# K products of an S4 layer on TensorE: two channels in one 64x66 product instead of one channel in a 32x33 product

## The chip, the cores and the metric

One core of a Trainium2 chip runs the kernel; the other cores are not used. The metric is the device time of one execution in microseconds (us), and runs are compared by their medians. The engines are named as in the profile: PE (TensorE; its weight loads are listed apart as PEld), DVE (VectorE), ACT (ScalarE), POOL (GpSimd) and SP (SyncE, which here only issues DMAs).

## The reference, cut to what matters

The output mixes two branches with a gate: `out = g * a + (1 - g) * b`, for 2048 positions and 640 channels, in bf16. Branch `a` is an S4 layer: for each channel a kernel K of 2048 taps is computed from 128 complex modes, and the input is convolved with it. Branch `b` is a gated MLP with a 2048 x 2048 product over the positions.

```python
    logdA = dt * A                                             # A complex, (D, N) = (640, 128)
    P = jnp.exp(logdA[:, :, None] * l[None, None, :])          # l = 0 .. 2047
    K = jnp.einsum('dn,dnl,dn->dl', Cc, P, dB).real
...
    y = irfft(rfft(pad(u)) * rfft(pad(K)))[:L] + u * Dskip     # convolution, per channel
...
    z1, z2 = split(gelu(x @ w_in)); z2 = layernorm(z2)
    b = (z1 * (w_sp @ z2 + b_sp)) @ w_out
    g = sigmoid((x * gate_w).sum(-1))
```

## The kernel before, in words

K is never evaluated tap by tap. Tap l is split into a coarse and a fine part, so that exp(l * logdA) is a product of two table entries, and the sum over the 128 modes is a matrix product with the modes on the 128 partitions. For one channel the coarse table has 32 rows that are used (real and imaginary parts apart) and the fine table 33. Channel d of K is thus a 32 x 33 block: the real product (`ET[:, 0:32, d]` by `M2[:, :, d]`) plus the imaginary one (`ET[:, NA:NA+32, d]` by `E2[:, :, d]`), accumulated in PSUM.

The channels are processed in eight groups c = 0..7 of 80. For each group:

- `k_exps` (for four groups at a time) and `k_tables` (lines 973 to 1030) fill the tables in the tile `ET{z}`, z = c % 2. It holds E1, E2 and M2 as rows of 80 channels, so the entries of one channel lie 80 elements apart. This is work of DVE and ACT.
- `k_sub` (lines 1034 to 1058) does the products. The 80 channels are four quarters q of 20. A quarter has its own 32 output columns of the PE array (`tile_position=(0, 32 * q)`) and so its own 32 PSUM partitions. For i in 0..19 and q in 0..3 there are two matmuls, lines 1045 and 1046: weights 128x32, moving operand 128x33. That is 160 matmuls, and as many weight loads, for a group, all in one PE task. One PSUM tile `ps_k` (two banks, from the ring "two", which has two such tiles and serves most large products of the kernel) takes all of it. Two copies (lines 1054 and 1056), both on DVE or both on ACT, bring it to the SBUF tile `kf` in order of taps: 17 columns of the fine table one way, 16 in reverse.
- `k_store` (lines 1069 to 1085) adds the skip weights to tap 0 (line 1075) and writes K to DRAM: for each quarter one DMA to `KA_d` and one to `KB_d`, and one more for the last row. It is called for the groups 0 to 3 together, for 4 and 5, and for 6 and 7 (lines 1311, 1312). `kf` of the first six groups (480 channels, h = 0) and of the last two (160 channels, h = 1) is one SBUF tile each.

`k_expand(h)` then reads `KA_d` and `KB_d` with some 27 DMAs, `conv_s1(h)` transforms K, and `conv_s2`, `conv_vt` and `conv_i2` do the convolution. The other branch runs alongside: `sp_block(tb)`, tb = 0..7, is the product over positions (line 812: 128x128 weights, 256 moving columns, 112 matmuls for a block) and the output product (line 832); `z1_tile` (line 624) and `s1_u` (line 651) are further PE work of the same stretch.

The order of the work is written by a planner, class `Plan` (lines 125 to 317). Every task is added with an engine (or a choice of engines), a cost in us, tiles and keys that it reads and writes, and a bias. The planner simulates the engines, always takes the ready task with the largest remaining path plus bias, and emits the instructions in that order; each engine runs its own in that fixed order. The dictionary `TUNE` (lines 38 to 121) adds searched biases to groups of tasks. A K product is entered with a cost of 3.65 and starts in the plan no earlier than 4.0 after the one before it has ended.

Of the kernel before, what the change touches and what calls it, by code (L numbers as in the profile page):

```python
# [25 lines left out]
class Handle:  # L26
# [9 lines left out]


TUNE = {
    ('conv_s1', 15, ('g', 0)): -1398,
    ('conv_s1', 15, None): 3878,  # L40
    ('conv_s2', 35, ('h', 0)): 10715,
    ('conv_s2', 34, ('h', 0)): 12557,
    ('conv_s2', 34, ('h', 1)): 10661,
    ('conv_s2', 28, None): -730,
    ('conv_s2', 42, None): 11507,
    ('eights', 6, None): 22869,
    ('eights', 13, None): 9278,
    ('i2_out', 15, None): 2641,
    ('k_expand', 28, ('h', 1)): -13135,
    ('k_exps', 10, ('c', 4)): -5933,  # L50
    ('k_exps', 10, None): -2461,
    ('k_store', 13, ('h', 1)): -2592,
    ('k_store', 14, None): -14209,
    ('k_store', 6, None): 2313,
    ('k_tables', 31, ('c', 4)): 1745,
    ('k_tables', 31, None): 2593,
    ('k_tables', 32, ('c', 3)): -6618,
    ('k_tables', 32, None): -5389,
    ('k_tables', 41, ('c', 3)): -7569,
    ('k_tables', 29, ('c', 3)): 19395,  # L60
    ('k_tables', 29, ('c', 7)): 107,
    ('k_tables', 29, None): -29059,
    ('k_tables', 6, ('c', 2)): -1107,
    ('k_tables', 6, None): -36,
    ('k_tables', 18, ('c', 5)): 11204,
    ('k_tables', 18, None): 3646,
    ('k_tables', 17, ('c', 3)): -6816,
    ('k_tables', 17, None): 2377,
    ('k_tables', 36, ('c', 0)): 6700,
    ('k_tables', 36, ('c', 7)): -59230,  # L70
    ('k_tables', 36, None): -4043,
    ('k_tables', 38, None): -15448,
    ('main', 151, ('g', 0)): 41152,
    ('main', 151, ('g', 1)): 3118,
    ('main', 151, ('g', 2)): 1052,
    ('main', 149, None): 37766,
    ('main', 148, None): 1429,
    ('main', 147, None): 3632,
    ('main', 156, None): 2671,
    ('main', 159, None): -8713,  # L80
    ('main', 370, None): -17765,
    ('main', 369, None): -1820,
    ('main', 442, None): 125,
    ('main', 445, None): 3317,
    ('main', 413, None): -4292,
    ('quads', 10, None): 798,
    ('s1_u', 13, ('n0', 12)): -14799,
    ('s1_u', 13, ('n0', 2)): -11216,
    ('s1_u', 16, ('n0', 12)): -1100,
    ('s1_u', 16, ('n0', 2)): -2702,  # L90
    ('s1_u', 16, ('n0', 4)): -8304,
    ('s1_u', 16, None): -26814,
    ('s1_u', 20, ('h', 1)): 37644,
    ('s1_u', 3, ('n0', 0)): -28168,
    ('s1_u', 3, None): 2258,
    ('s1_u', 18, ('h', 1)): -33016,
    ('s1_u', 14, None): -24028,
    ('sp_block', 23, ('tb', 4)): -6232,
    ('sp_block', 23, None): 6779,
    ('sp_block', 25, None): 2910,  # L100
    ('sp_block', 20, ('tb', 0)): 13918,
    ('sp_block', 20, None): -32605,
    ('sp_block', 42, ('tb', 4)): -3738,
    ('sp_block', 42, ('tb', 5)): -4450,
    ('sp_block', 47, ('tb', 3)): 6173,
    ('sp_block', 3, ('tb', 1)): -8813,
    ('sp_block', 3, ('tb', 2)): 26644,
    ('sp_block', 3, ('tb', 7)): -26408,
    ('sp_block', 8, None): -13664,
    ('sp_block', 6, None): -1104,  # L110
    ('sp_block', 5, ('tb', 7)): -23479,
    ('sp_block', 5, None): -15147,
    ('tg_build', 15, None): 6085,
    ('tg_build', 20, None): 11595,
    ('x_group', 3, ('g', 0)): -1523,
    ('x_group', 3, ('g', 1)): -4918,
    ('x_group', 3, None): -1876,
    ('z1_tile', 10, ('g', 0)): 17523,
    ('z2_tile', 18, ('h', 1)): -43258,
    ('z2_tile', 10, None): -1119,  # L120
}
HELPERS = ("dma", "actf", "evac", "<lambda>", "ptt", "pts", "ftt", "fts", "pstt", "S_", "E", "K_", "M_")

# [197 lines left out]
def kernel(  # L321
# [20 lines left out]
    P = 128  # L342
# [132 lines left out]
        S_(dma("SP", lambda nm=nm: nat[nm][:], lambda ap=ap: ap, 163840, w=[nm] + (["nat_in"] if k == 3 else []), tr=True, bias=6900 - k))  # L475
    add("DVE", 0.2, lambda e: vec.memset(dsk[:], 0.0), w=["dsk0"], bias=8000)
    for h in range(2):
        dma("POOL", lambda h=h: dsk[0:128:32, (0, 120)[h]:(120, 160)[h]], lambda h=h: A_Dskip[GO[h]:GO[h] + GW[h]].rearrange("(q d) -> q d", q=4), 1000, r=["dsk0"], w=[("dsk", h)], bias=7000)
    dma("POOL", lambda: bs16[:], lambda: B_b_sp.rearrange("(p n) -> p n", n=NS), 4000, w=["bs16"], bias=8000)
    E(dma("SP", lambda: Win1[:], lambda: wiv[:, :, 0:Fh], 1106000, w=["Win1"], r=["nat_in"], bias=3500, run=1728))  # L480

# [550 lines left out]
    SQ = 20  # L1032

    def k_sub(h, s, kf):
        ps = two("ps_k")
        z = s % 2
        tabs = [(nm, z, g) for nm in ("M2p", "E2p") for g in range(2)] + [(nm, z) for nm in ("M2n", "M2z", "E2n", "E2z")] + [(nm, z, g) for nm in ("E1", "E1s") for g in range(3)]

        def m(e):
            ET, M2, E2 = X["ET", z], X["M2", z], X["E2", z]  # L1040
            for i in range(SQ):
                for q in range(4):
                    d = SQ * q + i
                    o_ = ps()[32 * q:32 * q + 32, i // 10, 33 * (i % 10):33 * (i % 10) + 33]
                    pe.matmul(o_, lhsT=ET[:, 0:32, d], rhs=M2[:, :, d], start=True, stop=False, tile_position=(0, 32 * q))  # L1045
                    pe.matmul(o_, lhsT=ET[:, NA:NA + 32, d], rhs=E2[:, :, d], start=False, stop=True, tile_position=(0, 32 * q))  # L1046
        tab_ids.append(add("PE", 3.65, m, r=tabs + (["cva"] if h else []), w=[ps], bias=8000, lag=[(tab_ids[-1], 4.0)] if tab_ids else []))
        pv = lambda: ps()[:, :, 0:330].rearrange("p g (i b) -> p b g i", b=33)
        WQ = GW[h] // 4

        def ev(e):
            cp = vec.tensor_copy if e == "DVE" else act.copy
            kv = kf()[:, 0:33 * WQ].rearrange("p (b d) -> p b d", b=33)
            cp(out=kv[:, 16:33, SQ * s:SQ * s + 20].rearrange("p b (g i) -> p b g i", g=2), in_=pv()[:, 0:17, :, :])
            src = kv[:, 15, SQ * s:SQ * s + 20]
            cp(out=bass.AP(src.tensor, src.offset, [list(src.ap[0]), [-WQ, 16], [10, 2], [1, 10]]), in_=pv()[:, 17:33, :, :])
        i_ = add(("ACT", "DVE"), (0.9, 0.91), ev, r=[ps], w=[(kf, s)], bias=8500)
        K_(h, i_)

    QQ = ("SP", "POOL")  # L1060

# [7 lines left out]
    def k_store(h, kf, s0, s1):  # L1069

        WQ = GW[h] // 4
        c0, c1 = SQ * s0, SQ * s1
        o = (0, 120)[h]
        ks = [(kf, s) for s in range(s0, s1)]
        add("DVE", 0.25, lambda e: vec.tensor_tensor(out=kf()[:, c0:c1], in0=kf()[:, c0:c1], in1=dsk[:, o + c0:o + c1], op=ALU.add),
            r=[("dsk", h)] + ks, w=ks, bias=9000)
        kv = lambda: kf()[:, 0:33 * WQ].rearrange("p (b d) -> p b d", b=33)
        for q in range(4):
            cs = slice(WQ * q + c0, WQ * q + c1)
            r0 = 32 * q  # L1080
            KAB[h] += [("KA", h, q, s0), ("KB", h, q, s0)]
            K_(h, dma(QQ, lambda cs=cs: KA_d[h][:, :, cs], lambda r0=r0: kv()[r0:r0 + 16, :, c0:c1], 1056 * (c1 - c0), r=ks, w=[KAB[h][-2]], bias=8000, run=2 * (c1 - c0)))
            K_(h, dma(QQ, lambda cs=cs: KB_d[h][0:128, cs].rearrange("(a b) d -> a b d", a=4), lambda r0=r0: kv()[r0 + 16:r0 + 20, 0:32, c0:c1], 256 * (c1 - c0), r=ks, w=[KAB[h][-1]], bias=8000, run=2 * (c1 - c0)))
        KAB[h].append(("KC", h, s0))
        K_(h, dma(QQ, lambda: KB_d[h][128, :].rearrange("(q d) -> q d", q=4)[:, c0:c1], lambda: kv()[19:128:32, 32, c0:c1], 640, r=ks, w=[KAB[h][-1]], bias=8000))

    def k_expand(h):
        W = GW[h]
# [210 lines left out]
    sp_block(1)  # L1299
    for c in range(8):  # L1300
        h = c // 6
        if c == 0:
            kf[0] = sbt(KGP, "kf0", "kf0", [P, 33 * 120])
        if c == 6:
            kf[1] = sbt(CVA, "kf1", "kf1", [P, 33 * 40])
        if c in (0, 4):
            phase[0] = k_exps(c, 4)
            sids = []
        sids += k_tables(c)
        k_sub(h, c % 6, kf[h])  # L1310
        if c in (3, 5, 7):
            k_store(h, kf[h], *{3: (0, 4), 5: (4, 6), 7: (0, 2)}[c])
        if c in (1, 5):
            del z1_ids[:]
            xg = x_group(2 + c // 4)
            for f0 in range(0, NFT, 2):
                z1_tile(f0, 2 + c // 4, xg, sids[-6:-5], sids)
            phase[0], sids = list(z1_ids), []
        elif c in (3, 7):
            phase[0], sids = sids, []  # L1320
        if c == 5:
            for i in range(8):
                s1_u(2 * i)
            add("NONE", 0.0, open_cva, w=["cva", "al", "be"], deps=early_ids, r=["HT", "br_d", "gwt", "bt16", "phi"])
        if c == 5:
            xk, wk = k_expand(0)
            conv_s1(0, xk, wk)
# [49 lines left out]
```

## Time and profile before

| | before |
|---|---|
| median of 3 runs | 353.0 us (352.21 to 354.79) |
| profiled execution, its own time | 354.05 us |
| its span, first to last instruction | 352.3 us |
| mean granted TensorE clock | 0.967 |
| PE busy | 312.7 us, 3231 matmuls |
| DVE busy | 285.1 us |
| ACT busy | 245.2 us |
| POOL busy | 86.3 us |
| DMA | 59.89 MB in 108580 packets, 75914 of them under 512 B |

Busy time counts a stretch once, however many instructions overlap in it. The page names groups by line, engine and operation with their busy time, the mean duration of one instruction, and what ended the idle time before them. Matmuls overlap, so the distance between the starts of two is what one costs, and not its duration. The chain of waits follows the end of the execution back, at each step to what released it. The timeline gives start and length of runs of equal instructions, the count behind the x.

### The profile page before, as it was taken

To read this page: it belongs to the slowest core of one execution; us is meant where nothing else is said; L and a number is where in the kernel's file an instruction comes from. 1 tells how busy PE (TensorE), PEld (TensorE's weight loads), DVE (VectorE), ACT (ScalarE), POOL (GpSimd) and SP (SyncE) were. 2 spreads that over 40 slices of the span, in tenths; PEclk is the share of its full clock that TensorE was granted. 3 is DMA by queue.
4 is the path that set the end of the run, shared out by engine and by line. 5 is a ranking of instruction groups with operands and counts; after the bars stand their busy time and mean duration, and the time that the engine had idled before them with its cause. 6 is when DMAs were issued, how large, how long until landed. Compare 5 with 4: busy or idle time off the path is not lost.

```text
span 352.3 us, 8350 instructions
## 1 busy us (share of the span) xinstructions
PE 312.7 (89%) x3231; PEld 218.7 (62%) x3237; DVE 285.1 (81%) x560; ACT 245.2 (70%) x440; POOL 86.3 (25%) x107
## 2 busy tenths in 40 slices
PE   3899899989999999999999999699999999709982
PEld 3455455767766877878866988476774334406751
DVE  4079996799899599993799699327669999996985
ACT  1877648999996489999986671327558879604842
POOL 3007242000000041000440063427459200303220
PEclk9999999999999999999899999699999999976998
DMA  7979878788575596686296249989869866372404
GB/s 197 209 135 233 173 195 210 206 144 212 168 186 143 112 181 190 162 198 207 78 117 173 82 61 135 163 231 251 241 186 288 245 199 177 97 220 95 141 28 130
DMA packets 108580, 59.89 MB, mean 170 GB/s; under 512 B 75914, under 2 KB 105002, under 8 KB 108542
## 3 DMA queue, kind: packets, MB, share of 16 engines
q1 hardware_dynamic: 106030, 54.89, 63.9%
q0 software_dynamic: 2512, 4.48, 6.2%
q8 instruction: 25, 0.41, 0.5%
q14 instruction: 13, 0.11, 0.1%
HBM read 25.25 MB, written 19.47 MB: 127 GB/s over the span
## 4 chain that ended last, share of the span: by engine, by line
PE 49%; DVE 20%; ACT 13%; SPq 6%; issue 4%; DMA 4%; ACTq 0%; DVEq 0%
PE ps_g L812 21%; PE ps_o L832 6%; SPq L408 6%; PE ps_z L624 6%; ACT mr L415 5%; DVE p L1190 5%; DVE vs L1204 5%; PE ps_k L1046 3%; PE ps_k L1045 3%; PE ps_s2k L1188 3%; PE ps_v L1196 2%; DVE bst L604 2%; PE ps_s1k L1134 2%; ACT ET L415 1%; ACT L415 1%
## 5 line engine op out<-in xcount | busy, mean ns | idle before, releaser
L812 PE MATMUL ps_g<-wT,z2n 128*128 128x256 bf16 (+1 forms) x896 | 109.2, 278 | 1.7 <-DVE vT L816 1.2
L812 PEld LDWEIGHTS <-z2n 128*128 128x128 bf16 (+1 forms) x896 | 90.8, 104 | 18.7 <-issue 3.9
L1190 DVE TENSOR_TENSOR p<-ps_s2k,us 128x960 bf16<-128x960 f32 (+1 forms) x48 | 48.3, 1042 | 2.0 <-PE ps_s2k L1188 1.0
L993 POOL COPY ET<-mr 128x80 bf16<-128x80 bf16 x7 | 9.8, 1407 | 133.0 <-PE ps_k L1046 126.9
L832 PE MATMUL ps_o<-Wout,vT 128*128 128x320 bf16 (+1 forms) x224 | 33.8, 299 | 0.9 <-DVE vT L818 0.5
L624 PE MATMUL ps_z<-xg,Win 128*128 128x512 bf16 (+1 forms) x134 | 31.2, 379 | 1.4 <-ACT gl L598 1.1
L415 ACT ACTIVATE ET<-ci 128x640 bf16<-128x640 int16 (+1 forms) x40 | 25.7, 678 | 9.5 <-DVE ci L361 9.5
L592 PE MATMUL ps_z<-Win,xT 128*128 128x432 bf16 (+1 forms) x160 | 31.1, 353 | 1.0 <-ACT gl L598 1.0
L1046 PE MATMUL ps_k<-ET 128*32 128x33 bf16 x640 | 28.4, 258 | 3.9 <-issue 3.8
L1046 PEld LDWEIGHTS <-ET 128*32 128x32 bf16 x640 | 27.7, 195 | 3.3 <-issue 3.2
L1045 PEld LDWEIGHTS <-ET 128*32 128x32 bf16 x640 | 27.3, 192 | 2.6 <-issue 1.9
L1045 PE MATMUL ps_k<-ET 128*32 128x33 bf16 x640 | 28.8, 259 | 0.0
L832 PEld LDWEIGHTS <-vT 128*128 128x128 bf16 (+1 forms) x224 | 21.7, 97 | 10.2 <-issue 1.0
L1198 ACT CAST vs<-ps_v 128x480 bf16<-128x480 f32 (+1 forms) x48 | 24.4, 524 | 5.0 <-PE ps_v L1196 4.1
L1196 PE MATMUL ps_v<-p,G 128*128 128x480 bf16 (+1 forms) x128 | 25.2, 303 | 1.6 <-DVE p L1190 0.8
L816 DVE TENSOR_TENSOR vT<-ps_g,br 128x512 bf16<-128x512 f32 (+1 forms) x32 | 19.1, 617 | 8.6 <-PE ps_g L812 8.6
L1188 PE MATMUL ps_s2k<-fk,T 128*128 128x480 bf16 (+1 forms) x128 | 25.1, 306 | 0.2
L592 PEld LDWEIGHTS <-xT 128*128 128x128 bf16 x160 | 15.8, 99 | 15.3 <-issue 2.3
L415 ACT ACTIVATE mr<-lre 128x320 bf16<-128x320 f32 x66 | 25.0, 458 | 0.3 <-DVE ET L1017 0.2
L422 ACT CAST us<-ps_u 128x480 bf16<-128x480 f32 (+1 forms) x48 | 24.1, 523 | 0.8 <-ACT vs L1198 0.6
L624 PEld LDWEIGHTS <-Win 128*128 128x128 bf16 (+1 forms) x140 | 14.2, 101 | 16.1 <-issue 1.4
L422 ACT CAST s1k<-ps_s1k 128x960 bf16<-128x960 f32 (+1 forms) x15 | 13.0, 890 | 16.0 <-PE ps_s1k L1134 5.7
(192 smaller groups left out, 585.1 us busy)
## 6 DMA issues: line engine op xcount, KB each, us to landing
FU_d<-s1u SPq DMA_DIRECT2D x16, 240.0 KB, 3.0
fu<-FU_d SPq DMA_DIRECT2D x16, 240.0 KB, 2.9
fk<-FK_d SPq DMA_DIRECT2D x16, 240.0 KB, 3.0
z_d<-zt SPq DMA_DIRECT2D x24, 128.0 KB, 2.0
z1t<-z_d SPq DMA_DIRECT2D x8, 384.0 KB, 4.6
xf<-in_A_u_dram SPq DMA_DIRECT2D x8, 320.0 KB, 3.4
FK_d<-s1k SPq DMA_DIRECT2D x5, 480.0 KB, 5.4
Win<-in_B_w_in_dram SPq DMA_DIRECT2D x2, 1080.0 KB, 6.0
```

The source lines that it names most:

```text
L415: return add("ACT", cost, lambda e: act.activation(out=out_(), in_=in_(), func=func, scale=scale), r=r, w=w, fset=fs, bias=bias, deps=deps ...
L422: (vec.tensor_copy if e == "DVE" else act.copy)(out=out_(), in_=in_())
L592: pe.matmul(ps()[:, h, 0:432 + h], lhsT=xT[:, i, 128 * st:128 * st + 128], rhs=Win2[:, i, 432 * h:432 * h + 432 + h], start=(i == 0), stop ...
L624: pe.matmul(ps()[0:fs, ft - f0, :], lhsT=Win1[:, i, 128 * ft:128 * ft + fs], rhs=xg()[:, i, :], start=(i == 0), stop=(i == ND - 1))
L812: pe.matmul(ps()[0:fs, ft - f0, :], lhsT=z2n[:, st, 128 * ft:128 * ft + fs], rhs=wT()[:, st, :], start=(st == 0), stop=(st == NS - 1))
L832: pe.matmul(ps()[:], lhsT=vT[ft // 2]()[0:fs, ft % 2, 128 * r:128 * r + 128], rhs=Wout[0:fs, ft, HD * h:HD * h + HD], start=(ft == 0), sto ...
L1045: pe.matmul(o_, lhsT=ET[:, 0:32, d], rhs=M2[:, :, d], start=True, stop=False, tile_position=(0, 32 * q))
L1046: pe.matmul(o_, lhsT=ET[:, NA:NA + 32, d], rhs=E2[:, :, d], start=False, stop=True, tile_position=(0, 32 * q))
L1188: pe.matmul(ps()[:, i, W * n:W * n + W], lhsT=TK(k + n, i), rhs=fk()[:, j + n, :], start=True, stop=True)
L1190: add("DVE", dv1(2 * NW), lambda e, p12=p12, ps=ps, us=us: vec.tensor_tensor(out=p12()[:, :, 0:NW], in0=ps()[:, :, 0:NW], in1=us()[:, 0:NW ...
L1196: pe.matmul(pv()[:, W * n:W * n + W], lhsT=GV(k + n, i), rhs=p12()[:, i, W * n:W * n + W], start=(i == 0), stop=(i == 1))
L1198: add("ACT", 0.15 + NW / 1170, lambda e, k=k, pv=pv: act.copy(out=X["vs"][h][:, k:k + NK, :], in_=pv()[:, 0:NW].rearrange("p (k d) -> p k ...
```

## The change: what it does

One product now covers two channels of a group, d and d + 40. The weights are 64 columns: the 32 rows of the table of both channels, interleaved (row 0 of d, row 0 of d + 40, row 1 of d, ...), which is one access pattern with a step of 40 elements. The moving operand is 66 columns: 33 of d, then 33 of d + 40. The 64 x 66 result holds the blocks of both channels and the two mixed blocks, which mean nothing. It occupies half the columns of the array, so there are two positions p in place of four.

- `k_sub` makes two PE tasks (hf = 0, 1), each with a PSUM tile of its own, of 10 x 2 x 2 = 40 matmuls (weights 128x64, 66 moving columns) and two copies. A group has 80 matmuls and four copies in place of 160 and two. Each task is entered in the plan with a cost of 1.2 and with a distance of 1.3 (second half) or 4.0 (first half) from the end of the one before.
- The copies take the whole result, mixed blocks included, so `kf` has a second index a over 66 rows. `kf` keeps its size but holds three groups (h = 0) or one (h = 1): a new `kf` of the same ring, which has one place, is taken at c = 3 and at c = 7.
- `k_store` is called at c = 2, 5, 6 and 7. It picks the valid half by taking every second partition and the row index a that belongs to it. Its last-row DMA becomes two, so a store has ten DMAs instead of nine. The skip weights are loaded to other partitions by four small DMAs instead of two, and added to both halves.
- `TUNE` is replaced as a whole; the order of all tasks is that of a new search.

```diff
 TUNE = {
-    ('conv_s1', 15, ('g', 0)): -1398,
...
+    ('conv_i2', 39, None): -8406,
...
     def k_sub(h, s, kf):
-        ps = two("ps_k")
...
-            for i in range(SQ):
-                for q in range(4):
-                    d = SQ * q + i
-                    o_ = ps()[32 * q:32 * q + 32, i // 10, 33 * (i % 10):33 * (i % 10) + 33]
-                    pe.matmul(o_, lhsT=ET[:, 0:32, d], rhs=M2[:, :, d], start=True, stop=False, tile_position=(0, 32 * q))
-                    pe.matmul(o_, lhsT=ET[:, NA:NA + 32, d], rhs=E2[:, :, d], start=False, stop=True, tile_position=(0, 32 * q))
-        tab_ids.append(add("PE", 3.65, m, r=tabs + (["cva"] if h else []), w=[ps], bias=8000, lag=[(tab_ids[-1], 4.0)] if tab_ids else []))
...
+        for hf in range(2):
+            ps = two("ps_k")
+            def m(e, hf=hf, ps=ps):
+                ET, M2, E2 = X["ET", z], X["M2", z], X["E2", z]
+                for i in range(10):
+                    for p in range(2):
+                        d0 = SQ * p + 10 * hf + i
+                        ds = slice(d0, d0 + 2 * SQ + 1, 2 * SQ)
+                        st = lambda r0: bass.AP(ET.tensor, ET[:, r0, d0:d0 + 1].offset, [list(ET[:, r0, d0:d0 + 1].ap[0]), [2 * SQ, 64]])
+                        o_ = ps()[64 * p:64 * p + 64, i // 5, 66 * (i % 5):66 * (i % 5) + 66]
+                        pe.matmul(o_, lhsT=st(0), rhs=M2[:, :, ds].rearrange("p b q -> p q b"), start=True, stop=False, tile_position=(0, 64 * p))
+                        pe.matmul(o_, lhsT=st(NA), rhs=E2[:, :, ds].rearrange("p b q -> p q b"), start=False, stop=True, tile_position=(0, 64 * p))
+            tab_ids.append(add("PE", 1.2, m, r=tabs + (["cva"] if h else []), w=[ps], bias=8000 + 500 * hf, lag=[(tab_ids[-1], 1.3 if hf else 4.0)] if tab_ids else []))
+            def ev(e, hf=hf, ps=ps):
+                cp = vec.tensor_copy if e == "DVE" else act.copy
+                pv = ps()[:, :, 0:330].rearrange("p g (i a b) -> p b a g i", a=2, b=33)
+                kv = kf()[:, 0:66 * WK].rearrange("p (b a d) -> p b a d", b=33, a=2)
+                cc = c0 + 10 * hf
+                cp(out=kv[:, 16:33, :, cc:cc + 10].rearrange("p b a (g i) -> p b a g i", g=2), in_=pv[:, 0:17, :, :, :])
...
     def k_store(h, kf, s0, s1):
...
-        K_(h, dma(QQ, lambda: KB_d[h][128, :].rearrange("(q d) -> q d", q=4)[:, c0:c1], lambda: kv()[19:128:32, 32, c0:c1], 640, r=ks, w=[KAB[h][-1]], bias=8000))
+            K_(h, dma(QQ, lambda cs=cs: KA_d[h][:, :, cs], lambda r0=r0, q=q: kv()[r0:r0 + 32:2, :, q // 2, l0:l1], 1056 * (c1 - c0), r=ks, w=[KAB[h][-2]], bias=8000, run=2 * (c1 - c0)))
...
+        for a in range(2):
+            KAB[h].append(("KC", h, s0, a))
+            K_(h, dma(QQ, lambda a=a: KB_d[h][128, :].rearrange("(q d) -> q d", q=4)[2 * a:2 * a + 2, c0:c1], lambda a=a: kv()[38 + a:128:64, 32, a, l0:l1], 320, r=ks, w=[KAB[h][-1]], bias=8000))
...
-        if c == 0:
+        if c in (0, 3):
             kf[0] = sbt(KGP, "kf0", "kf0", [P, 33 * 120])
-        if c == 6:
+        if c in (6, 7):
             kf[1] = sbt(CVA, "kf1", "kf1", [P, 33 * 40])
...
-        if c in (3, 5, 7):
-            k_store(h, kf[h], *{3: (0, 4), 5: (4, 6), 7: (0, 2)}[c])
+        if c in (2, 5, 6, 7):
+            k_store(h, kf[h], *{2: (0, 3), 5: (3, 6), 6: (0, 1), 7: (1, 2)}[c])
```

## The prediction, made before the changed kernel was run

> **What bounds the kernel now.** I read the page's busy times and chain first:
>
> ```profile
> PE 312.7 (89%) x3231; PEld 218.7 (62%) x3237; DVE 285.1 (81%) x560; ACT 245.2 (70%) x440; POOL 86.3 (25%) x107
> PE 49%; DVE 20%; ACT 13%; SPq 6%; issue 4%; DMA 4%; ACTq 0%; DVEq 0%
> ```
>
> PE has half the chain. The stages of the K products (first at 116.6 us, last at 237.2), from the table of windows (PE, PEld, DVE, ACT, POOL, then clock and DMA):
>
> ```profile
> 116.00:140.00 24.00, 22.78 (x448) 19.10 (x447) 19.64 (x50) 18.78 (x32) 5.74 (x2) 1.00 0.78 165
> 140.00:165.00 25.00, 25.00 (x341) 21.06 (x340) 19.90 (x31) 23.90 (x48) 0.25 (x1) 1.00 0.74 192
> 165.00:190.00 25.00, 24.10 (x296) 18.45 (x297) 21.77 (x53) 21.20 (x36) 7.58 (x8) 0.93 0.63 127
> 190.00:215.00 25.00, 24.92 (x465) 21.24 (x464) 21.65 (x50) 15.52 (x26) 6.52 (x9) 1.00 0.51 84
> 215.00:240.00 25.00, 21.94 (x412) 16.88 (x411) 12.94 (x21) 6.70 (x9) 10.82 (x17) 0.86 0.92 199
> ```
>
> PE is busy for 118.7 of 124 us; DVE sums to 95.9 and ACT to 86.1, so they have 28 and 38 us free. A microsecond more or less of PE moves the end of this stretch by nearly as much. What a product costs is in the timeline of the first group (start, length; x4 is four instructions that start within some 15 ns):
>
> ```profile
> 115.83 0.82 PE L812 MATMUL ps_g<-wT,z2n 128*128 128x256 bf16 x6
> ...
> 116.57 0.29 PE L1045 MATMUL ps_k<-ET 128*32 128x33 bf16 x4
> ...
> 116.67 0.28 PE L1046 MATMUL ps_k<-ET 128*32 128x33 bf16 x4
> ...
> 117.69 0.21 PEld L1045 LDWEIGHTS <-ET 128*32 128x32 bf16 x4
> 117.76 0.27 PE L1045 MATMUL ps_k<-ET 128*32 128x33 bf16 x4
> 117.78 0.21 PEld L1046 LDWEIGHTS <-ET 128*32 128x32 bf16 x4
> 117.84 0.27 PE L1046 MATMUL ps_k<-ET 128*32 128x33 bf16 x4
> 117.86 0.21 PEld L1045 LDWEIGHTS <-ET 128*32 128x32 bf16 x4
> ...
> 119.83 0.28 PE L1046 MATMUL ps_k<-ET 128*32 128x33 bf16 x4
> ...
> 120.05 2.14 PE L812 MATMUL ps_g<-wT,z2n 128*128 128x256 bf16 x18
> ```
>
> The code issues both products of quarter 0, then both of quarter 1, and so on. The array runs them otherwise: four loads together, some 62 ns later four matmuls together, some 20 ns after these the next four loads. So the four column tiles run side by side, and each goes through load, product, load, product in series. The beat is (119.83 - 116.67) / 38 = 83.2 ns. It is there from the second beat on, though PE's queue could fill during the slow products before it (256 columns each). That speaks for a chain in each tile, not for a limit on issue.
>
> A group has 20 x 2 = 40 beats, 3.33 us. The last product of line 812 starts at 116.38 (115.83 + 0.82 less a 0.27 duration) and its successor was due about 0.11 later, at 116.49; the next such product starts at 120.05. So the block takes 3.57 us, 0.24 of it for getting in and out. The second group, at 124.15, gives the same.
>
> **What the Trainium skill says.** (1) "TensorEngine Tiling (Array Packing)", Key Properties: tiles load and multiply in parallel, and changing the tiling mode drains the engine. The trace agrees: fours start together, and a block loses 0.24 us at its edges. (2) "TensorE: Matmul & The Clock Gate", LDWEIGHTS: a load takes its columns divided by 1.2 ns, so 32 columns more are an estimated 27 ns. The trace has no 64-column load. (3) The same page, Back-to-back issue gap: no product of up to 64 columns below about 25 ns. Here a pair costs 83.2 / 4 = 20.8 ns, so with tiles that floor does not hold. (4) The tiling page, PSUM Bottleneck: tiling does not speed up evacuation; here the copies double.
>
> **The change, part by part.**
>
> Beats. Before, each of four tiles has 40 pairs a group; after, each of two tiles has 40 pairs. Halving the matmuls halves the tiles, not the length of the chain, and each link grows. Weights: +27 ns by (2), or +13 if loads run at double that rate. Moving columns: line 1196 takes 367 ns with 480 columns and 240 with 160, 0.40 ns each, so 33 more are +13. Two starts in a burst instead of four: two times about 4 ns less, -8. I take 83.2 + 27 + 13 - 8 = 115 ns. Ends: 72 (latency alone counts and the burst shrinks) and 166 (all of it doubles).
>
> Edges. A group is two tasks with other work between, so 0.24 is paid twice. A group costs 2 x (20 x 0.115 + 0.24) = 5.08 us against 3.57, +1.51, and eight groups +12.1 us. At 72 ns it is 3.36 each, -1.7 in all; at 166, 7.12 and +28. Break-even is 77 ns.
>
> Copies. DVE takes 0.82 us for a pair (120.21 to 121.03), ACT 0.75; eight more pairs are about 6.3 us. I take none of it on the path: 28 us of DVE and 38 of ACT are free in the stretch. Without that cover it is all 6.3. The finer interleave (runs of 5 instead of 10) keeps the element count; I take the same price.
>
> PE's hole. The chain has this line inside group 6:
>
> ```profile
> 221.02 3.06 issue
> ```
>
> PE waits for nothing that the profile shows, among 320 short instructions; the change issues 160 there. It may go (-3.1) or stay (0); I take -1.5.
>
> `kf` taken anew at c = 3. Its copies must wait until the ten DMAs of the store have landed: five on each queue at 0.65 us, and 5.7 to land (median of these stores), 9 us after the last copy of c = 2. In the trace before, the copies of c = 2 end at 163.5 and those of c = 3 begin at 172.5, 9 us later. So it just fits: 0, at worst 3 us, when both PSUM tiles of the ring hold K results and the large products behind them on PE stand. At c = 7 the small stores have 11.8 us (225.7 to 237.6): 0.
>
> Stores. 40 DMAs instead of 27, at 0.6 to 0.7 us each on SP and POOL. POOL is 25% busy and SP waits for most of its issues on other engines, so this is hidden, except that the store before `k_expand(0)` has ten instead of nine: 0 to 0.7, taken 0. About 2,600 packets more, of 108,580: nothing. The four loads of the skip weights, the wider addition of line 1075 and early POOL work: nothing, hidden under the same idle time.
>
> The order. All of it is new, and the old trace can't price that. It holds a half to be much shorter than 2.54 us, so copies and stores planned behind it come late; 0 to 5 us, taken 0, since PE works in the meantime. A gain of up to 3 from PE's other idle time isn't excluded.
>
> Sum, against the profiled execution: 352.3 + 12.1 - 1.5 = 362.9 span, 1.75 more around it, 364.6. That execution stands 1.05 above the median of 353.0, so 363.5 is the median that I forecast.
>
> **Rivals.**
>
> A. Chain length stays (+1.9 us). If the 62 ns from load to product are latency and the loads come through one path, two loads of 64 columns cost what four of 32 do, and the beat stays at 83. Only the edges are added: 8 x 0.24 = 1.9. With the hole that is 353.4, from 352 to 357. For it: 128 columns of weights a beat, before and after. Against it: the next load starts only after the product, so its length should count.
>
> B. Faster: PE is bound by issuing pairs at 20.8 ns. Then 80 pairs are 1.66 us, a group 1.66 + 0.48 = 2.14, eight groups -11.4, with the hole -12.9: 340. As the products also wait for tables, which DVE and ACT fill in 80 and 70% of the stretch while they get 6.3 us of copies, I expect a half to all of it: 340 to 347, so 344. Against it: starts in fours and the beat at once at 83. It decides where the two-tile beat is below 77 ns.
>
> C. Slower still: the chain as forecast, and `kf` or the mis-estimated order stalls PE by 5 us or more: 369 to 378. For it: 9 us against 9 us at c = 3.
>
> **How the numbers follow.** Forecast 0.45 (359 to 369), A 0.22, B 0.20, C 0.13. The range from 344 to 370 leaves out half of B and most of C, about 2 in 10. The runs before spread over 0.7%, so 1%, 3.5 us, is about what can be told from no change. Faster by over 1%: B and a little of A, 0.22. Within: most of A, 0.17. Slower: the forecast, C and the rest of A, 0.61.
>
> **What would show it.** In the changed profile, 640 products with a beat, read from starts of equal bursts of two, near 115 ns: 83 is A, about 42 is B. Blocks of 20 beats near 2.5 us, sixteen of them; 16 pairs of copies of 0.75 to 0.82 us; PE above 95% busy in the stretch. A gap on PE after the products of c = 3, ended by copies that waited for the store's DMAs, is C. A beat below 77 makes the forecast wrong.

## The result, and the profile after

The changed kernel takes 368.2 us (median of 4 runs, 366.09 to 369.52) beside 353.5 us for the kernel before on the same chip (4 runs, 352.21 to 354.79): ratio 1.041, 95% interval 1.035 to 1.048. Forecast were 363.5, and a range of 344 to 370. The profiled execution took 366.09 us with a span of 364.3; it is the shortest of the four, so the spans lie only 12.0 apart and the medians 14.8. The ratios below leave out executions over 1.5% longer than the fastest of the same kernel, which are few but for run e4: there they are 10 of 17, and the median of all 17, 355.9 us, is no better than the 355.2 of the kernel before.

The page of the changed kernel has PE's busy time up by 12 us, with 2597 matmuls where there were 3231, DVE's unchanged and ACT's up by 5.5:

```profile
PE 324.6 (89%) x2597; PEld 229.4 (63%) x2597; DVE 285.2 (78%) x564; ACT 250.7 (69%) x454; POOL 81.6 (22%) x111
```

Its chain of waits adds up to only 39% of the span, because it breaks off early, so I don't set its shares beside the old ones. The timeline of the first block of products (start, length, the count behind the x):

```profile
115.69 1.47 PE L830 MATMUL ps_g<-wT,z2n 128*128 128x256 bf16 x12
117.09 0.38 PE L1068 MATMUL ps_k<-ET 128*64 128x66 bf16 x2
117.29 0.32 PE L1069 MATMUL ps_k<-ET 128*64 128x66 bf16 x2
117.42 0.32 PE L1068 MATMUL ps_k<-ET 128*64 128x66 bf16 x2
...
119.65 0.31 PE L1069 MATMUL ps_k<-ET 128*64 128x66 bf16 x2
119.89 0.58 PE L669 MATMUL ps_s<-xf,F 128*128 128x480 bf16 x2
```

From 117.29 to 119.65 are 18 beats: 131 ns each, where 83 were before and 115 forecast. The last product of line 830 starts 0.28 before its group ends, at 116.88, and its successor was due 0.11 later, at 116.99; the next product starts at 119.89. The block takes 2.90 us, a group 5.80, where it was 3.57: eight groups are 8 x 2.23 = 17.8 us of PE.

The windows of the stretch (columns as before) say the same in another way:

```profile
140.00:165.00 25.00, 25.00 (x264) 21.95 (x263) 18.85 (x34) 19.79 (x38) 3.40 (x5) 1.00 0.60 122
165.00:190.00 25.00, 25.00 (x219) 19.67 (x218) 21.89 (x50) 22.21 (x44) 0.00 (x0) 1.00 0.69 175
190.00:215.00 25.00, 25.00 (x256) 19.50 (x254) 15.76 (x38) 15.15 (x24) 1.38 (x3) 1.00 0.26 74
```

In these three rows PE has no hole at all and its clock is 1.00; DVE sums to 56.5 us and ACT to 57.2, where they had 63.3 and 60.6. PE alone sets the pace there.

Why does the span grow by 12.0 and not by 17.8? Before, PE's two holes in the products (`issue: 3.8, 2, 3.1` in its waits: 3.8 us in two, the longest 3.1) were each followed by a stretch of half clock. This is the window table of the kernel before, microsecond by microsecond, around the second one; the clock is the third column from the end:

```profile
221.00:222.00 1.00, 0.02 (x1) 0.00 (x0) 0.17 (x1) 0.80 (x2) 1.00 (x3) 1.00 1.15 187
222.00:223.00 1.00, 0.00 (x0) 0.00 (x0) 0.00 (x0) 0.00 (x0) 0.34 (x1) 1.00 1.12 122
223.00:224.00 1.00, 0.00 (x0) 0.00 (x0) 0.00 (x0) 0.00 (x0) 0.00 (x0) 0.71 1.33 184
224.00:225.00 1.00, 0.93 (x21) 0.81 (x22) 0.19 (x1) 0.00 (x0) 0.22 (x1) 0.50 0.83 191
...
229.00:230.00 1.00, 1.00 (x4) 0.45 (x3) 0.00 (x0) 0.34 (x1) 0.00 (x0) 0.50 0.74 76
230.00:231.00 1.00, 1.00 (x8) 0.69 (x7) 0.97 (x1) 0.00 (x0) 0.00 (x0) 0.88 0.94 196
```

PE is back at 224 and has half the clock until after 230: up to 3.1 us lost (six slices at 0.50, one at 0.88). The same table around the first hole has 0.61, 0.50, 0.50 and 0.68 from 172 to 176: 1.7 us more. In the changed kernel both holes and both slow stretches are gone, 3.8 + 4.8 = 8.6 us, and one wait is new, of products of line 1161 for the expanded K:

```profile
PE ps_s1k L1161 <- DMA xk<-KA_d: 3.6, 2, 3.3
```

17.8 - 8.6 + 3.3 = 12.5 us, against 12.0 measured. The page agrees in sum: PE's busy time is up by 11.9, and its idle time is 39.6 before and 39.7 after.

### The profile page after: what moved, and what is told of

It reads as the page before. It is cut to its first block, busy times and chain, and to the rows that moved or that the text cites. A ratio compares the mean times of both kernels' runs of the same rounds, so it can differ in the third digit from the quotient of the medians.

```text
span 364.3 us, 7132 instructions
## 1 busy us (share of the span) xinstructions
PE 324.6 (89%) x2597; PEld 229.4 (63%) x2597; DVE 285.2 (78%) x564; ACT 250.7 (69%) x454; POOL 81.6 (22%) x111
## 5 line engine op out<-in xcount | busy, mean ns | idle before, releaser
L830 PE MATMUL ps_g<-wT,z2n 128*128 128x256 bf16 (+1 forms) x896 | 105.7, 273 | 3.4 <-DVE vT L834 3.3
L830 PEld LDWEIGHTS <-z2n 128*128 128x128 bf16 (+1 forms) x896 | 88.5, 101 | 18.9 <-issue 6.4
L1068 PE MATMUL ps_k<-ET 128*64 128x66 bf16 x320 | 44.2, 320 | 0.0
L1069 PE MATMUL ps_k<-ET 128*64 128x66 bf16 x320 | 43.0, 314 | 0.0
L1068 PEld LDWEIGHTS <-ET 128*64 128x64 bf16 x320 | 34.6, 204 | 4.0 <-issue 3.2
L1069 PEld LDWEIGHTS <-ET 128*64 128x64 bf16 x320 | 34.9, 206 | 0.1
L834 DVE TENSOR_TENSOR vT<-ps_g,br 128x512 bf16<-128x512 f32 (+1 forms) x32 | 18.8, 617 | 12.1 <-PE ps_g L830 9.9
L610 PEld LDWEIGHTS <-xT 128*128 128x128 bf16 x160 | 15.4, 97 | 17.8 <-issue 3.9
L427 POOL DMA_DIRECT2D KA_d<-kf x8 | 5.6, 697 | 88.8 <-DVE ai L979 55.7
L432 ACT ACTIVATE zt<-ps_z 128x1024 bf16<-128x1024 f32 (+1 forms) x16 | 14.6, 917 | 13.6 <-PE ps_z L642 7.6
```

Source lines behind the costliest of these rows:

```text
L432: return add("ACT", cost, lambda e: act.activation(out=out_(), in_=in_(), func=func, scale=scale), r=r, w=w, fset=fs, bias=bias, deps=deps ...
L610: pe.matmul(ps()[:, h, 0:432 + h], lhsT=xT[:, i, 128 * st:128 * st + 128], rhs=Win2[:, i, 432 * h:432 * h + 432 + h], start=(i == 0), stop ...
L830: pe.matmul(ps()[0:fs, ft - f0, :], lhsT=z2n[:, st, 128 * ft:128 * ft + fs], rhs=wT()[:, st, :], start=(st == 0), stop=(st == NS - 1))
L1068: pe.matmul(o_, lhsT=st(0), rhs=M2[:, :, ds].rearrange("p b q -> p q b"), start=True, stop=False, tile_position=(0, 64 * p))
L1069: pe.matmul(o_, lhsT=st(NA), rhs=E2[:, :, ds].rearrange("p b q -> p q b"), start=False, stop=True, tile_position=(0, 64 * p))
```

## The experiments

Theory at the outset: the product's form alone makes the loss, by its longer beat. Rivals: the copies and stores, the doubled PSUM tiles and the new order. All ratios are to the kernel before on the same chip, with 95% intervals.

| run | what it is | ratio to before |
|---|---|---|
| e1_old_products | changed kernel, products 32 x 33 again | 1.001 (0.996 to 1.005) |
| e2_new_products | kernel before, products 64 x 66 | 1.022 (1.016 to 1.029) |
| e3_copies_twice | changed kernel, each K copy done twice | 1.050 (1.045 to 1.055) |
| e6_true_cost_in_plan | changed kernel, planned with the true cost | 1.042 (1.035 to 1.049) |
| e4_close_tables | kernel before, tables in bundles of four channels | 0.990 (0.987 to 0.994) |
| e5_contiguous_operands | changed kernel, products read contiguous elements | 0.963 (0.957 to 0.968) |
| e7_pairs_close | changed kernel, the two channels of a pair adjacent | 1.049 (1.042 to 1.056) |
| e8_pairs_close_cost | e7, planned with a shorter product | 1.062 (1.056 to 1.068) |
| e9_pairs_step2 | changed kernel, pairs in bundles of four, step 2 | 0.981 (0.977 to 0.985) |

**Which part costs the time: e1, e2, e3, e6.** In e1 the changed kernel gets the old products back; the copies read each block twice:

```diff
-                    for p in range(2):
-                        d0 = SQ * p + 10 * hf + i
+                    for q in range(4):
+                        d = SQ * q + 10 * hf + i
...
-                        pe.matmul(o_, lhsT=st(0), rhs=M2[:, :, ds].rearrange("p b q -> p q b"), start=True, stop=False, tile_position=(0, 64 * p))
+                        pe.matmul(o_, lhsT=w0, rhs=M2d, start=True, stop=False, tile_position=(0, 32 * q))
```

> The changed kernel with its order, copies and stores, but each half does its 40 channels as four tiles of 32 weights and 33 columns (20 beats); the copies read each block twice, so K is wrong, at the same number of copied elements. Theory (the beat is the whole loss): a half falls from 2.90 to 1.91 us on TensorE, 16 x 0.99 = 15.8 us less, so about 352 to 354. Rival (the order, searched with too short a cost, the doubled copies or the store that must land before the next K tile cost most of it): 360 or more.

Measured: 1.001. In sum, the whole rest of the change (two blocks a group, eight more pairs of copies, stores, `kf`, the order) costs nothing that can be measured. But the sum is a balance. The waits of PE in e1:

```profile
PE ps_s1k L1161 <- DMA xk<-KA_d: 3.8, 1, 3.8
PE ps_k L1069 <- issue: 0.9, 1, 0.9
```

The wait for the expanded K is there with the old products too, 3.8 us, and two blocks of 1.91 us cost 3.82 a group instead of 3.57, 2.0 in all. Against that, 2.9 of the 3.8 us of holes are gone, and half clock costs 1.7 us (behind the wait) instead of 4.8. That is 5.8 - 6.0 = -0.2 us; the span is 0.3 longer (352.6).

e2 is the other half, the new products in the kernel before:

```diff
-                for q in range(4):
-                    d = SQ * q + i
+                for p in range(2):
+                    d0 = SQ * p + i
...
+                    pe.matmul(o_, lhsT=st(0), rhs=M2[:, :, ds].rearrange("p b q -> p q b"), start=True, stop=False, tile_position=(0, 64 * p))
```

> The kernel before with its order, copies and stores, but each group's products in the form of two tiles with 64 weights and 66 moving columns (40 beats, results laid over one another in the one PSUM tile, so K is wrong). Theory: a group takes 40 x 0.131 + 0.29 = 5.53 instead of 3.57 us, +15.7 in all, so 369; if the holes in the products of groups 3 and 6 and the halved clock after them come from the many short instructions and go with them, 3 to 8 less, 361 to 366. Rival (order and copies are the loss): 357 or less.

Measured: 1.022, or 8.0 us; its span is 8.4 longer. The sign is as the theory has it, the size about half. With one block a group, the products cost 40 x 0.131 + 0.28 = 5.52 us instead of 3.57, 15.6 for eight. The rest is what this edit takes away: e2 has no wait for issue in its products, and its mean clock is 0.978 instead of 0.967. One stretch of half clock is left, at the end of a block and with PE busy throughout:

```profile
242.00:243.00 1.00, 1.00 (x20) 1.00 (x20) 0.00 (x0) 0.00 (x0) 0.00 (x0) 0.58 1.08 415
243.00:244.00 1.00, 1.00 (x20) 1.00 (x18) 0.00 (x0) 0.00 (x0) 0.00 (x0) 0.50 0.98 338
```

Its products keep their beat of 131 ns there (from 242.99 to 244.04 are eight), so only what follows them until 246 is slowed, by about 0.7 us. 15.6 - 8.6 + 0.7 = 7.7, against the 8.4.

So e1 and e2 do not add up to the change (0.1% and 2.2% against 4.1%): most of the holes and of their half clock goes in either of them, with the old form in the new order and with the new form in the old order, and can go only once. In the new order, from e1 to the changed kernel, the form costs 1.0411 / 1.0008, that is 4.0%.

In e3 each copy is made twice:

```diff
-                cp = vec.tensor_copy if e == "DVE" else act.copy
+                cp = lambda **kw: [(vec.tensor_copy if e == "DVE" else act.copy)(**kw) for _ in range(2)]
```

> The changed kernel with each copy of the K results to SBUF done twice. Theory: DVE and ACT have room, 16 more pairs of 0.8 to 0.9 us (14 us of engine time) cost 0 to 3 us, 368 to 371. Rival (copies are on the path): 375 or more.

Measured: 1.050. By the groups of the changed kernel, eight pairs on DVE at 507 + 480 ns and eight on ACT at 444 + 438 are 15.0 us of engine time. Doubling them moves the time by 0.9% of 353, 3.2 us, and the intervals of the two ratios overlap. So some four fifths of the copies are hidden.

In e6 the planner is given what a half really takes:

```diff
-            tab_ids.append(add("PE", 1.2, m,
+            tab_ids.append(add("PE", 2.9, m,
```

> The changed kernel, planned with 2.9 us for a half instead of 1.2, the searched biases kept; the order of all engines comes out anew. Theory (the products are the loss, the order does not matter): within 3 us of the changed kernel, 365 to 371. Rival (the order that expected short products causes waits): 360 or less.

Measured: 1.042, no different from the 1.041 of the change. The mis-estimate in the plan is not what costs, as long as the searched biases stay; a new search with the true cost was not tried.

**What makes the beat: m1 and m2.** These kernels leave out the whole layer and only issue blocks of products on tables of fixed data: 40 beats on equal terms, each kernel run once. The beats of a block belong to two lines in turn, so from the first to the last start of one line are 38 of them. The figures below are worked out from starts to 0.01 us in the timeline.

> No part of the layer: only runs of 20 small products of each shape on TensorE, between dense products, and an output of zeros. What is read is the beat, the distance between starts of bursts. Theory (each tile runs load, product, load, product in series, and both lengths count): four tiles with 32 weights and 33 columns 83 ns as in the kernel before; 66 columns instead of 33 adds about 14 ns, 120 columns about 36; two tiles with 64 weights and 33 columns 83 + some 27 to 35; two tiles with 64 and 66 about 131 as in the changed kernel; two of four tiles, 32 and 33: 83 still. Contiguous operands and another issue order change nothing. Rival (one shared path for loads, or a limit on issue): two of four tiles takes about half, 42 to 45, and two tiles with 64 weights and 33 columns stays at 83. Rival (the step between elements in SBUF costs): the contiguous forms are clearly shorter. Without tiles, 128 weights load behind the products, so 132 columns should take about 60 to 70 ns and 33 columns no less than about 55.

The lines of m1 (ns min/median/max, then first and last start in us; weights, then moving operand):

```profile
L42 PE MATMUL ps_k<-T x80: 252/258/284, 21.7 to 24.9; 128*32 128x33 bf16 x80
L69 PE MATMUL ps_k<-T x40: 311/313/379, 45.4 to 50.5; 128*64 128x66 bf16 x40
L78 PE MATMUL ps_k<-T x80: 177/188/191, 53.6 to 54.9; 128*32 128x33 bf16 x80
L87 PE MATMUL ps_k<-T x40: 192/196/218, 57.7 to 59.0; 128*64 128x66 bf16 x40
L122 PE MATMUL ps_k<-T x80: 241/247/292, 91.3 to 94.5; 128*32 128x120 bf16 x80
```

L42 and L69 are the products of the two kernels: 84 and 132 ns (83 and 131 in the kernels). In L78 and L87 the same shapes read contiguous elements: 33 to 34 ns both. Shape alone makes no difference; the step between the elements of a table row in SBUF does. In the two kernels a product's rows lie 80 elements apart, or 40 in the interleaved weights. Two tiles instead of four at the old shape gave 84, another issue order 84 and 133. L122 has the weights of L42 but 120 contiguous columns instead of 33 strided ones: 84 ns as well, where the series of load and product had 36 more.

m2 gives weights and moving operand steps of their own:

```diff
-                pe.matmul(o_, lhsT=st(0, d, 80, 32), rhs=mv(73, d, [[80, 33]]), ...
+                pe.matmul(o_, lhsT=st(0, d, 80, 32), rhs=mv(73, d, [[1, 33]]), ...
```

> Again only runs of 40 beats of each form, no part of the layer. In the first such run the beat of both forms fell to 33 ns with contiguous operands, so the step between elements is the cost, and my series of load and product is in doubt. New theory (loads and products overlap, the longer one sets the beat, and each costs per element according to its step): 32 weights at step 80 with contiguous columns 82 ns; contiguous weights with 33 columns at step 80 about 65 (132 columns took 251, so 1.9 to 2.0 each); 64 weights at step 40 with contiguous columns about 118; contiguous weights with 66 columns at step 80 about 131, the same as with both strided, so that in the changed kernel the moving operand is the limit and in the kernel before the weights. Old theory (series): contiguous weights with 66 strided columns clearly below 131. With steps 2 to 64 for both operands: if only what lies in one short line of SBUF is read at once, the beat rises with the step up to some width and is flat beyond; if any step costs, it is 83 from step 2 on.

```profile
L42 PE MATMUL ps_k<-T x80: 228/235/253, 22.3 to 25.5; 128*32 128x33 bf16 x80
L51 PE MATMUL ps_k<-T x80: 223/249/250, 30.2 to 32.7; 128*32 128x33 bf16 x80
L60 PE MATMUL ps_k<-T x40: 282/286/305, 37.4 to 42.0; 128*64 128x66 bf16 x40
L69 PE MATMUL ps_k<-T x40: 290/313/316, 46.8 to 51.8; 128*64 128x66 bf16 x40
L87 PE MATMUL ps_k<-T x80: 191/196/208, 63.5 to 64.9; 128*32 128x33 bf16 x80
L96 PE MATMUL ps_k<-T x80: 243/250/264, 69.6 to 72.2; 128*32 128x33 bf16 x80
```

L42 has only the weights at step 80: 84 ns. L51 has only the moving operand at step 80: 66. Together they take 84, not 150: load and product of successive beats overlap, and the longer sets the beat. For the pair it is the same: weights alone at step 40 take 120 (L60), the moving 66 alone 130 (L69), both 132. So the weights were the limit before and the moving operand is now. L87 has both at step 4, 37 ns, and L96 both at step 8, 68; with 16, 32 and 64 it stays at 61 to 68.

Per moving column that is about 2.0 ns at step 8 and above (130 / 66, 66 / 33), 1.0 at step 4 (65 ns for 66 columns, line 132) and 0.5 at most when contiguous (33 / 66): about 2 ns for every 16 bytes of SBUF touched. A weight at step 80 takes 84 / 32 = 2.6. The Trainium skill, "Advanced Engine Details and Errata", SBUF Cachelines, says that SBUF has lines of 16 bytes, that accesses to the same line run at full rate and that an access to another line each time is penalized. The runs agree, with the end of the rise at 8 elements, which are 16 bytes. It also says that at least two hits on a line are needed to hide the access time; step 4 has two, and still costs at least twice what contiguous reading does, so two are not enough here.

**Is the step all of it: e4 and e5.** e5 is the changed kernel with both operands taken from neighbouring elements of the same tile:

```diff
-...[2 * SQ, 64]])
+...[1, n]])
-                        pe.matmul(o_, lhsT=st(0), rhs=M2[:, :, ds].rearrange("p b q -> p q b"), ...
+                        pe.matmul(o_, lhsT=st(0), rhs=st(2 * NA + 33 + i, 66), ...
```

> The changed kernel with everything but the addresses that its products read: 64 weights and 66 columns that lie next to each other in the same table tile, so K is wrong. Theory (the step of the operands is the whole loss): the beat falls from 131 to about 33 ns, a half from 2.90 to 0.9 us, 32 us less of TensorE; the stretch is then bound by the tables on DVE and ACT, so not all of it comes: 338 to 348. Rival (the form itself, the edges of the blocks or the order cost the time): 360 or more.

Measured: 342.5 us, 0.963. With nothing but the addresses of its operands changed, the changed kernel goes from 4.1% slower to 3.7% faster. e4 is the old form with its step shortened the other way, by the layout: the tables are `[P, 20, 106, 4]`, so that four channels lie together and a row's elements are four apart. All tasks keep their order:

```diff
-            ET = pools["kg"].tile([P, 2 * NA + 66, SD], BF, name=f"ET{z}")
+            ET = pools["kg"].tile([P, SD // 4, 2 * NA + 66, 4], BF, name=f"ET{z}")
```

> The kernel before in its own order and with its own products, but the tables lie in groups of four channels: the entries of a channel are 4 elements apart instead of 80. Theory (the step sets the beat): 40 beats of about 36 ns, a group 1.44 + 0.25 = 1.7 instead of 3.57 us on TensorE, 15 less in all. If DVE and ACT write and read runs of four elements at the old price, 340 to 345 (part of the gain is lost to waits for tables); if VectorE loses its double rate there, its products of tables take 4 to 5 us more a group, some 36 in all against 28 free, and the time is 353 or more. Rival (the number of pairs or the issue sets the product's cost): no change on TensorE, 353.

Measured: 0.990 by the shorter of its executions, and no gain by all of them, where 340 to 345 us were hoped for. The products' busy time falls from 28.8 and 28.4 us to 13.8 and 13.5, and DVE's table operations keep their price. But holes take the place; the waits of PE in e4:

```profile
PE ps_k L1046 <- issue: 8.9, 3, 4.5
PE ps_k L1045 <- ACT zt L415: 3.4, 1, 3.4
```

(The traced execution took 357.1 us, so nothing is read from its span.) The holes come in kernels with 320 loads and products in a group: before (3.8 us), e1 (0.9, though in two blocks of 160), e4 (8.9, at the shortest beat). With 160 of them in a group, in the changed kernel, e2, e5, e7 and e9, no product waits for issue. Of the blocks of 320 in m1 and m2 only one has a hole, of 0.8 us (line 79 of m2). That the instructions arrive too slowly is my reading; no run isolates it.

**A layout that keeps K: e7, e8, e9.** e7 puts the two channels of a pair side by side, tables `[P, 40, 106, 2]`, so that weights and moving operand are each one contiguous stretch:

```diff
+            ET = pools["kg"].tile([P, SD // 2, 2 * NA + 66, 2], BF, name=f"ET{z}")
+                        st = lambda r0, n=32: ET[:, d0, r0:r0 + n, :].rearrange("p r f -> p (r f)")
```

> The changed kernel with its order and its 64 x 66 products, but the two channels of a product lie next to each other in the tables (the channels of a group are permuted once, where the parameters are prepared), so that 64 weights and 66 columns are each one contiguous run. Unlike the run with contiguous operands before, K is the one wanted. Theory (the step was the loss): beat about 33 ns, as there; DVE and ACT write runs of two elements at the old price, as they did runs of four; the split preparation costs up to 2 us. So 341 to 346. Rival (runs of two elements take VectorE's double rate): its products of tables take some 4 us more a group and the time is 355 or more.

Measured: 1.049, the rival's side. Its products are fast, but the groups of DVE show who pays (busy us, mean ns):

```profile
L1046 DVE TENSOR_TENSOR ET<-ET,mr 128x3200 bf16<-128x3200 bf16 x8 | 25.1, 3139 | 0.0
L1035 DVE TENSOR_TENSOR ET<-ET,mr 128x2560 bf16<-128x2560 bf16 x8 | 20.4, 2562 | 0.6 <-ACT mr L432 0.5
```

They took 1818 and 1485 ns in the changed kernel. With this layout, in runs of two elements, DVE takes 1.7 times as long; its busy time rises by 29 us to 314.2, and PE waits 14.2 us for ET. e8 plans this kernel with a product cost of 0.95 instead of 1.2:

> As the run before, planned with 0.95 us for a half instead of 1.2, the biases kept. Theory (the order matters little where PE is no longer stretched): within 3 us of the run before.

Measured: 1.062, 377.2 us against 371.8 of e7, so not within the 3 us: the order does matter there, and the shorter planned cost is no help.

e9 puts the two together: bundles of four as in e4, where DVE kept its rate, and a pair made of the entries x and x + 2 of a bundle, so that the operands have step 2:

```diff
-            ET = pools["kg"].tile([P, SD // 2, 2 * NA + 66, 2], BF, name=f"ET{z}")
+            ET = pools["kg"].tile([P, SD // 4, 2 * NA + 66, 4], BF, name=f"ET{z}")
-                        st = lambda r0, n=32: ET[:, d0, r0:r0 + n, :].rearrange("p r f -> p (r f)")
+                        st = lambda r0, n=32: (lambda t: bass.AP(t.tensor, t.offset, [list(t.ap[0]), [2, 2 * n]]))(ET[:, d0 // 2, r0, d0 % 2:d0 % 2 + 1])
```

> The changed kernel with its tables laid out so that both sides should be served: the channels of a group lie in 20 bundles of four ([P, 20, 106, 4]), a product takes the entries x and x + 2 of a bundle, so that its 64 weights and its 66 moving elements each lie two elements apart in one stretch, and DVE and ACT write and read runs of four. K is right, the order of all tasks is that of the changed kernel. Theory (the cost of a product follows the step between its elements; runs of two, not of four, cost DVE its rate): a beat near 33 ns, blocks of 20 beats near 1.0 us, table operations at their old 1.8, 1.5 and 0.8 us, and a median of 341 to 349, that is 0.965 to 0.99 of the kernel before; above 342.5 by what the finer preparation of the permuted channels costs (some more small operations on DVE before 60 us). Rival 1 (the close tables pay on DVE or ACT whatever the run): table operations above 2.3 us, PE waits for tables, 358 or more. Rival 2 (step 2 is slower than step 1 where a column tile is 64 wide): a beat of 65 ns, blocks of 1.6 us, 349 to 355.

Measured: 347.3 us (6 runs, 346.96 to 348.0), 0.981, a little faster than the kernel before; against the changed one it is 0.9811 / 1.0411 = 0.942. Its first block in the timeline, and DVE's largest group:

```profile
118.56 0.23 PE L1068 MATMUL ps_k<-ET 128*64 128x66 bf16 x2
118.61 0.20 PE L1069 MATMUL ps_k<-ET 128*64 128x66 bf16 x2
...
119.22 0.20 PE L1069 MATMUL ps_k<-ET 128*64 128x66 bf16 x2
119.35 0.58 PE L669 MATMUL ps_s<-xf,F 128*128 128x480 bf16 x2
```

```profile
L1046 DVE TENSOR_TENSOR ET<-ET,mr 128x3200 bf16<-128x3200 bf16 x8 | 14.5, 1816 | 0.0
```

The beat is (119.22 - 118.56) / 19 = 35 ns, and the table operation has its old price. 16 x 20 x (131 - 35) ns = 31 us of PE are saved over the changed kernel, and 21 of them arrive at the end. In the traces it is 18.3 of span: PE's busy time falls by 27.4, since 3.4 are lost again to half clock behind two of its waits, and its idle time rises by 9.1, of which 2.9 are waits for the tables (ET).

## Why the prediction was right, and where it was not

**Sign, size and range** were right: slower, 368.2 in 344 to 370. But that it is only 4.7 us from the forecast is luck: the sum has larger misses of both signs.

**The beat, the term that was mis-sized.** 115 ns forecast, 131 measured; a group 5.08 and 5.80 us. The 131 lie within the bounds of 72 and 166. The argument behind the 115, "each goes through load, product, load, product in series", fell in m2: the beat is the longer of the two, 84 where the sum would be 150. The starts in the old timeline (a load some 20 ns after the product, a product 62 ns after the load) fit both readings, and I took one without bounding the other. It came out near because the wrong mechanism and the wrong prices (27 ns for 32 more weights, 13 for 33 more columns) partly cancel: 32 more weights cost 36 ns (84 to 120), 33 more columns 64 (66 to 130), and the second does not come on top of the first. Neither price has a step in it: the page names none, and line 1196 reads neighbouring elements; that the table rows lie 80 elements apart stands in the description of the kernel and was not used. It would have put the 66 moving columns in question at once.

**Edges.** 0.24 forecast, 2.90 - 20 x 0.131 = 0.28 measured: right.

**PE's hole.** -1.5 forecast, half of the 3.1; all of it went, with the smaller hole and the half clock behind each: up to -8.6. The half clock was in the prediction's own fence, 0.93 and 0.86 in the clock column, and not priced. The Trainium skill, "TensorE: Matmul & The Clock Gate", Why this matters for your kernels, warns that idle gaps beyond about 3 us bring the slow clock back. The 3.06 us hole agrees. But the 0.79 us hole was followed by slow clock too, while the 3.3 us wait of the changed kernel (1.00 in each slice behind it), two holes of 2.5 and 1.8 us in e4 and the one of 0.8 in m2 were not; and in e2 and m1 (0.50 from 42 to 45 us) the clock fell with PE busy throughout. So the length of the gap alone doesn't decide here, that the holes brought the half clock is not shown, and what does decide stays open.

**Copies, stores, `kf`, order.** All taken at nothing on the path, and e1 has them together at 1.001, though as a balance of the new wait and the second edges with the holes that are gone. That is rival A's 353.4, within the interval, but with the old form: A's beat of 83 ns did not come with the new one. A pair of copies costs what it did, 507 + 480 ns on DVE (511 + 480 before) and 444 + 438 on ACT (433 + 428), mostly hidden as e3 shows. For `kf` the copy at c = 3 did wait, 3.2 us for the stores' DMAs on DVE, the worst case named, but PE has none of it. What the order did cost is the 3.3 us wait for the expanded K; e1, e3, e5, e7 and e9 have it too (3.4 to 4.0 us), whatever their products. It lies in the 0 to 5 that were named and taken 0, and below the 5 of rival C.

**Rival B** (issue of pairs at 20.8 ns) is excluded for these kernels: contiguous four-tile blocks ran a beat of four pairs in 33 to 34 ns, some 8 each. Its outcome is real for other addresses: e5 ended at 342.5, where B had 344.

**In sum,** by terms against the forecast's 12.1 - 1.5 = 10.6: products +17.8 (5.7 more), holes and clock -8.6 (7.1 more), order +3.3 (0 taken), so 12.5 against a measured span difference of 12.0. The rest up to 14.8 in the medians is where the profiled executions lie: 2.1 us below the median of the changed kernel, and 0.6 above that of the kernel before.

## What to carry to other kernels

Before costing a small product, write down the step between the elements of each operand in SBUF: here about 2 ns a column at 16 bytes or more, at most a quarter of that when contiguous, and the wider product paid it on the side that was not the limit before. Take the longer of load and product, as in m2, and not their sum, unless a run shows otherwise. A layout that serves TensorE has to serve the engine that fills the table as well: bundles of four channels did for both, with the operands at step 2, and bundles of two for one only.

## What the runs showed of the hardware that was not expected

- With four column tiles and contiguous operands, a pair of load and product costs about 8 ns (33 / 4), and 64 x 66 products on two tiles have the same beat, 33 ns.
- Untiled, 128 weights at step 20 with 33 moving columns at step 80 gave a beat of 68 ns, what the 33 columns alone explain (66): the load of 128 columns did not show the 2.6 ns a weight of the narrow tiles.
- DVE's tensor product of bf16 keeps its rate in the tables with runs of four elements (1816 ns for 3200, as in the old layout) and not in those with runs of two (3139).
- Products with strided operands keep their beat when PE has half the clock: 131 ns in e2 at 1.00 and at 0.50, and 258 ns in m1 for untiled products with 132 strided columns (lines 113 and 114, 79.6 to 87.4 us) at both. The 24 dense products before a block of m1 took 2.7 us at 1.00 (from 55.0) and 4.4 where the clock was mostly 0.50 (from 41.0). That fits a limit in the reading of the operands and not in the array.
- The clock fell to 0.50 behind a hole of 0.79 us in the kernel before, not behind one of 0.82 in m2, and without any hole in e2 and m1.
